# A new instruction order for the head of a fused attention and gated-FFN kernel: softmax of batch 0 by halves, other PSUM banks, three weight visits exchanged

## The chip, the core and the metric

The kernel runs on one core of a Trainium2 chip. The core has a matrix engine (TensorE, PE in the profile) and three others that work on tiles: VectorE (DVE), ScalarE (ACT) and GpSimd (POOL). SyncE (SP) issues transfers; ACT and POOL issue some too. Each engine takes its instructions in the order in which the program gives them to it, and waits at an instruction until what it reads is there and what it overwrites is no longer needed. The metric is the device time of one execution in microseconds (us); less is better.

## What is computed

Two stages. The first is a pair of cross attentions, for 8 batches and 8 heads, between x (512 rows of 64) and a state (32 rows of 64):

```
a     = softmax(scale * x  @ state^T);   xread = a  @ state
a2    = softmax(scale * state @ x^T);    sread = a2 @ x
y     = concat(xread, sread)             # 544 rows per batch, heads side by side: 4352 x 512
```

The second is a gated FFN over those rows, with 512 inner and 1536 hidden columns:

```
out = (sigmoid(y @ w_gate) * (y @ w_val)) @ w_out
```

## The kernel before, in words

The whole kernel is scheduled by hand: the order of the calls in the program is the order on each engine's queue, and the tile framework adds the waits. There are eight PSUM banks, each a pool with one buffer, named G0, G1, OU, S0, S1, S2, S3 and AT; a call takes the bank it is to write as an argument, and waits until the last reader of that bank is done.

Attention and FFN are fused. Since xread is a linear map of the softmax weights, the kernel multiplies the state with w_gate and w_val once per batch (a *visit*, `sw_visit` at L297: eight matmuls for 256 columns of both weights, or 512 columns of one, into two banks, halves e = 0 and 1), copies the result to SBUF as `SW` (`sw_cp` at L328), and then multiplies `SW` with the transposed weights `aT`. `sw_wide` (L311) makes three visits in a row for batch 2.

The names that the order speaks of, for a batch b:

- `load_xp`, `load_xh` load parts of x; `cast_xp` (L93) makes bf16 of it. `xT_mm` (L126) transposes x on TensorE into a bank, `xT_cp` (L134) copies it out. `warm` (L600) issues 128x512 matmuls on zeros that nobody reads.
- `sT_mm`, `sT_pad`, `sT_cp` (L621 to L639) transpose the state and copy it out.
- `Sq_mm`, `Sq_exp`, `nq_sum`, `nq_mul` (L170 to L194) are scores, exponentials, row sums with reciprocals, and the division, for a quarter of batch 0 (two heads). `S_mm`, `S_exp`, `n_sum`, `n_mul` (L142, L164, L206, L223) are the same for a half (four heads).
- `aT_mm` (L230) transposes the divided weights `ab` on TensorE, `aT_cp` copies them out; from batch 2 on `aT_dma` does it by transposing transfers on SP, and `at_xT_dma` (L137) does it for x.
- `at_Eb` (L196) makes bf16 of the exponentials on POOL, and `rd_mm` (L253) multiplies them with x for the second attention: 32 matmuls, and 8 with a column of ones for the row sums. `rd_fin` (L270) divides.
- `gv_mm(b, f, gate bank, value bank)` (L335) is a unit of the gated FFN: for 128 hidden columns, two matmuls for the gate and two for the value. `gv_half` (L350) is the one or the other alone. `gv_th` (L361) takes tanh of the gate on ACT into a tile `th`, of which there are three buffers, and `gv_glu` (L366) joins gate and value on DVE.
- `h_mm`, `h_sum`, `ht_sum` (L448, L464, L467) multiply the result for batch 0 with w_out in seven products of 2x2 blocks instead of eight, with sums of blocks made on DVE and POOL. `load_wo(q)` loads a third of w_out; every product reads all three thirds or sums of them.

The head of the program, from L650 to L924, works on batches 0 and 1 and prepares batch 2; this is the part that is laid out anew. Behind it, `step(b, f)` (L971) runs over batches 2 to 7 in a fixed pattern of twelve units each, and is not touched. `step` begins with three visits and then a half unit that writes bank G1.

Of the kernel before, what the change touches and what calls it, by code (L numbers as in the profile page):

```python
# [16 lines left out]
def kernel(  # L17
# [75 lines left out]
    def cast_xp(b, cp, lo, n):  # L93
        xh_tile(b)
        cp(xhs[b][:, lo:lo + n], xfs[b][:, lo:lo + n])
# [504 lines left out]
    def warm(n, place):  # L600

        ps = place[0].tile((128, 512), FP, name="warm", tag=place[1])
        for _ in range(n):
            nc.tensor.matmul(ps.rearrange("p (r k) -> p r k", r=4), wm, wm.unsqueeze(1).to_broadcast((128, 4, 128)), start=True, stop=True)  # L604
# [50 lines left out]
    nc.vector.memset(wm, 0.0)  # L655
# [23 lines left out]
    load_w(0, 256, 256)
    load_w(1, 256, 256)  # L680
    Sq_mm(0, 0, S2)
    load_w(0, 1024, 256)
    Sq_exp(0, 0)
    xT_cp(0, 1, vec)
    Sq_mm(0, 1, AT)
    xT_mm(0, 3, S3)
    xT_mm(1, 0, S0, 2)
    nq_sum(0, 2)
    load_w(1, 1024, 256)
    xT_cp(0, 3, act)  # L690
    load_sb(2)
    Sq_mm(0, 3, OU)
    Sq_exp(0, 1)
    nq_sum(0, 0)
    nq_sum(0, 1)
# [45 lines left out]
    sw_cp(1, 1024, 2, 0, act)
    aT_mm(1, S0)
    gv_glu(0, 3)
    aT_cp(1, None, vec)
    gv_mm(0, 2, S2, S1)
    gv_th(0, 2)
# [1 line left out]
    gv_mm(0, 9, AT, S3)
    gv_mm(1, 3, G1, S0)
    gv_th(0, 9)  # L750
    sw_cp(1, 1024, 2, 1, vec)
    gv_mm(1, 2, AT, G0)
    gv_glu(0, 9)
    gv_th(1, 3)
    gv_glu(1, 3)
    nc.scalar.activation(pre[:, 0:1], ones, AF.Exp)
    gv_th(1, 2)
    sT_mm(2, S1)
    gv_mm(1, 8, S2, S3)
    zero(sTz, pool)  # L760
    gv_th(1, 8)
    gv_glu(1, 2)
    load_x(2, nc.gpsimd)
# [70 lines left out]
    sw_cp(2, 1, 2, 0, act)
    h_sum(0, 1, vec)
    gv_mm(1, 6, OU, S3)
    sw_visit(1, 1280, 256, S1, G0)
# [2 lines left out]
    sw_visit(1, 0, 256, S2, S0)  # L840
    sw_cp(1, 1280, 2, 0, act)
    h_sum(2, 0, pool)
    h_sum(2, 1, vec)
    sw_cp(1, 1280, 2, 1, act)
    gv_mm(1, 4, G1, OU)
    gv_glu(1, 6)
    cast_x(2, pool, 0, 4)
    gv_mm(1, 7, S1, AT)
    gv_th(1, 4)
    sw_cp(1, 0, 2, 1, vec)  # L850
    gv_glu(1, 4)
# [2 lines left out]
    gv_mm(1, 11, S3, G1)
    h_sum(1, 1, pool)
    gv_th(1, 11)
    at_xT_dma(2)
    gv_mm(1, 10, G0, S1)
    gv_glu(1, 11)
    h_mm(1, 0, AT)  # L860
    h_mm(1, 1)
    ht_sum(0, vec)
    h_sum(0, 0, pool)
    h_mm(5, 0, G1)
    S_mm(2, 0, OU)
    h_mm(5, 1)
    ht_sum(2, vec)
    h_sum(1, 0, vec)
    load_x(3, nc.sync)
    ht_sum(1, vec)  # L870
    gv_th(1, 10)
    h_mm(7, 0, S0)
    gv_glu(1, 10)
    sw_cp(1, 0, 2, 0, act)
    h_sum(3, 0, pool)
    w_keep('V1', 1)
    h_mm(6, 0)
    S_exp(2, 0)
    n_sum(2, 0)
    n_mul(2, 0, pool)  # L880
    S_mm(2, 1, G0)
    aT_dma(2, 0)
    S_exp(2, 1)
    gv_mm(1, 0, OU, S2)
    h_sum(3, 1, vec)
    gv_th(1, 0)
    h_mm(6, 1)
    w_keep('U2', 1)
    n_sum(2, 1)
    ht_sum(3, vec)  # L890
    n_mul(2, 1, pool)
    aT_dma(2, 1)
    h_U4()
    gv_mm(1, 1, G0, S1)
    h_mm(2, 0, S3)
    gv_glu(1, 0)
    h_mm(2, 1)
    gv_th(1, 1)
    cast_x(3, pool, 4, 4)
    h_mm(3, 0)  # L900
    gv_glu(1, 1)
    cast_x(3, pool, 0, 4)
    at_xT_dma(3)
    h_mm(7, 1)
    w_add(2, 'V1', w_res(0, 0)[:, :, lo_])
    h_mm(3, 1)
    sw_wide(2, 0, AT, S2, S1, G0, S3, OU)
    w_add(7, 'U4', w_res(0, 1)[:, :, hi_])
    sw_cp(2, 0, 1, 1, act)
# [286 lines left out]
```

## Time and profile before

| what | value |
|---|---|
| time, median of 3 runs | 211.4 us (211.23 to 212.68) |
| the profiled execution, its own time | 211.41 us |
| its span, first to last instruction | 209.6 us |
| DVE, ACT, POOL busy, 25 to 30 us | 4.75, 4.30, 2.49 us of 5 |
| DVE, ACT, POOL busy, 40 to 45 us | 4.96, 2.44, 2.82 us of 5 |

The profile page gives the busy time of each engine and its share of the span, then the chain of work that ended last. A view by stage cuts the span into stretches: each row has the stretch, its length, and for each engine the busy time with its number of instructions, then the granted clock, the share of the transfer engines and GB/s. Rows of the timeline have start, duration, engine, source line, operation, what is written and read, and in brackets how long the engine stood idle before it and what ended that. A row of the timeline merges neighbours of one kind (x4), and its duration is then that of the group. Groups of instructions have count, busy time and mean nanoseconds of one. Rows of transfers have the issuing queue, the size and the microseconds from issue to landing.

A duration of a matmul includes its way through the array, so neighbours overlap: what a matmul costs in a dense stretch is the pitch from start to start.

### The profile page before, as it was taken

Reading aid. Unit: us, or ns where it says so; the run is one execution under the profiler, and the core shown is the slowest. Engines: PE = TensorE matmul, PEld = TensorE weight load, DVE = VectorE, ACT = ScalarE, POOL = GpSimd, SP = SyncE. Lnnn points to the kernel's source line nnn. Section 1 sums busy time; section 2 is a strip of 40 time slices with the busy share of each in tenths; the row PEclk is TensorE's granted clock in tenths of the full one; section 3 lists DMA queues with packets and bytes.
Section 4 is the critical chain, followed back from the end, with each engine's and each line's share of the span. In section 5 each row is a group of like instructions: output and inputs, shape, how many; then the busy total and the mean of one; then the engine's idle time right before and its main releaser. Section 6 shows DMA issues by size and latency. Waiting matters only on the chain.

```text
span 209.6 us, 5504 instructions
## 1 busy us (share of the span) xinstructions
PE 202.9 (97%) x2161; PEld 132.8 (63%) x2161; DVE 172.1 (82%) x332; ACT 136.0 (65%) x257; POOL 79.7 (38%) x104
## 2 busy tenths in 40 slices
PE   7879999999999999999999999999999999999993
PEld 2545443677666656665666575666666777778982
DVE  1798899998997788668979898898978779798962
ACT  3978898753867467865786478648787566565420
POOL 8899458599041704900292028501600000000010
PEclk9999999999999999999999999999999999999998
DMA  6999999672689952995913440275020500022045
GB/s 206 186 192 191 226 278 183 113 213 42 78 208 337 141 103 77 308 119 161 299 45 60 105 170 16 44 99 206 13 47 0 204 1 3 0 85 118 2 156 147
DMA packets 40922, 27.17 MB, mean 130 GB/s; under 512 B 23616, under 2 KB 38720, under 8 KB 40896
## 3 DMA queue, kind: packets, MB, share of 16 engines
q1 hardware_dynamic: 30000, 18.95, 36.0%
q0 software_dynamic: 9920, 7.01, 20.5%
q10 hardware_dynamic: 976, 0.85, 1.3%
q8 instruction: 17, 0.28, 0.6%
q14 instruction: 9, 0.07, 0.1%
HBM read 18.35 MB, written 8.91 MB: 130 GB/s over the span
## 4 chain that ended last, share of the span: by engine, by line
PE 94%; DVE 2%; ACT 2%; issue 0%
PE gvp L355 30%; PE outp L434 29%; PE gvp L343 10%; PE gvs L531 4%; PE outp L454 4%; PE swp L286 4%; PE swp L293 2%; PE outp L571 2%; PE warm L604 2%; PE Sp L147 1%; PE outp L479 1%; PE rdp L262 1%; DVE rsq L186 1%; PE aTp L234 1%; ACT tw L638 1%; PE rdp L265 1%
## 5 line engine op out<-in xcount | busy, mean ns | idle before, releaser
L369 DVE SCALAR_TENSOR_TENSOR glu<-th,gvp 128x512 bf16<-128x512 f32 x96 | 64.9, 682 | 23.1 <-PE gvp L355 10.6
L364 ACT ACTIVATE th<-gvp 128x512 f32<-128x512 f32 x96 | 57.5, 603 | 35.2 <-PE gvp L355 32.4
L355 PE MATMUL gvp<-aT,SW 128*128 128x512 bf16 x288 | 77.5, 380 | 0.0
L329 ACT CAST SW<-swp 128x512 bf16<-128x512 f32 x83 | 46.6, 594 | 9.2 <-PE swp L286 8.3
L434 PEld LDWEIGHTS <-Sm 128*128 128x128 bf16 x324 | 31.3, 98 | 11.1 <-DVE Sm L414 0.2
L355 PEld LDWEIGHTS <-SW 128*128 128x128 bf16 x288 | 26.7, 98 | 17.0 <-issue 3.3
L200 POOL CAST Eb<-E 128x256 bf16<-128x256 f32 x32 | 13.9, 473 | 52.1 <-ACT E L167 52.1
L434 PE MATMUL outp<-tw,Sm 128*128 128x256 bf16 x240 | 31.4, 273 | 0.0
L434 PEld LDWEIGHTS <-glu 128*128 128x128 bf16 x240 | 23.2, 98 | 9.4
L434 PE MATMUL outp<-wo,glu 128*128 128x256 bf16 x168 | 22.8, 273 | 0.0
L343 PE MATMUL gvp<-aT,SW 128*128 128x512 bf16 x96 | 22.6, 380 | 0.0
L596 POOL DMA_DIRECT2D out_dram<-res x1 | 0.6, 613 | 50.1 <-ACT res L442 50.1
L227 POOL TENSOR_TENSOR ab<-E,ri 128x512 bf16<-128x512 f32 x13 | 14.3, 1101 | 10.6 <-DVE ri L210 6.0
L414 DVE TENSOR_TENSOR Sm<-glu 128x768 bf16<-128x768 bf16 x30 | 16.6, 559 | 0.0
L343 PEld LDWEIGHTS <-SW 128*128 128x128 bf16 x96 | 8.7, 98 | 10.5 <-issue 1.9
L445 DVE SCALAR_TENSOR_TENSOR res<-outp,U 128x512 f32<-128x512 f32 x20 | 13.6, 684 | 0.9 <-PE outp L454 0.9
L116 POOL CAST xb<-xf 128x1024 bf16<-128x1024 f32 x12 | 13.2, 1122 | 2.0 <-DMA xf<-in_x_dram 2.0
L167 ACT ACTIVATE E<-Sp 128x512 f32<-128x512 f32 x14 | 8.4, 599 | 6.7 <-PE Sp L147 5.8
L434 PE MATMUL outp<-wo,Sm 128*128 128x256 bf16 x84 | 11.3, 273 | 0.0
L251 POOL CAST xs<-xf 128x1024 bf16<-128x1024 f32 x10 | 10.1, 1040 | 0.0
L434 PE MATMUL outp<-tw,glu 128*128 128x256 bf16 x72 | 9.8, 273 | 0.0
L208 DVE TENSOR_REDUCE rs<-E 128x16 f32<-128x512 f32 x14 | 9.5, 677 | 0.2 <-ACT E L167 0.2
(124 smaller groups left out, 262.4 us busy)
## 6 DMA issues: line engine op xcount, KB each, us to landing
out_dram<-res SPq DMA_DIRECT2D x14, 512.0 KB, 3.2
xf<-in_x_dram SPq DMA_DIRECT2D x5, 1024.0 KB, 7.6
wo<-in_moe_w_out_dram POOLq DMA_DIRECT2D x3, 512.0 KB, 7.9
wgv<-in_moe_w_gate_dram POOLq DMA_DIRECT2D x4, 256.0 KB, 7.0
wgv<-in_moe_w_val_dram POOLq DMA_DIRECT2D x4, 256.0 KB, 8.3
xf<-in_x_dram POOLq DMA_DIRECT2D x1, 1024.0 KB, 9.5
xf<-in_x_dram SPq DMA_DIRECT2D x2, 256.0 KB, 3.9
xf<-in_x_dram ACTq DMA_DIRECT2D x2, 256.0 KB, 4.4
```

Of the source, the lines that this page charges most:

```text
L116: cp(xbs[b].rearrange("p c h d -> p h c d")[:, lo:lo + n], (xhs if b in xhs else xfs)[b][:, lo:lo + n])
L200: nc.gpsimd.tensor_copy(Ebs[b][:, c], E1s[b][:, c])
L227: (nc.gpsimd if eng is pool else nc.vector).tensor_tensor(half(b, i, abs_), e1, ri.unsqueeze(len(ri.shape)).to_broadcast(e1.shape), ALU.mult)
L251: pool(xs.rearrange("p c h d -> p h c d")[:, lo:lo + n, :, :D], xfs[b][:, lo:lo + n])
L329: cp(*sw_left.pop((b, lo, w, e)))
L343: nc.tensor.matmul(ps, SWs[b][:, g, w, fs], aTs[b][:, :, g], start=(g == 0), stop=(g == 1))
L355: nc.tensor.matmul(ps, SWs[b][:, g, w, fs], aTs[b][:, :, g], start=(g == 0), stop=(g == 1))
L364: nc.scalar.activation(th, held["gv", b, f][0], AF.Tanh, scale=0.5)
L369: nc.vector.scalar_tensor_tensor(glus[b][:, f], held["th", b, f], 1.0, held["gv", b, f][1], ALU.add, ALU.mult)
L414: eng.tensor_tensor(S_(b, t)[:, i], a, c, op)
L434: nc.tensor.matmul(wps[key][:, c], lhs[:, i, c * 128:(c + 1) * 128], rhs[:, i], start=(first and c == 0 and i == 0), stop=(i == NF // 2 - ...
L445: nc.vector.scalar_tensor_tensor(to, wps[key], 0.5, held["w", name], ALU.mult, ALU.add)
```

## The change

The functions keep what they do, except that `rd_mm` now issues the eight matmuls with ones ahead of the 32 others for batch 2, and as before behind them for batches 0 and 1. Everything else is the order of calls in the head and the arguments that name engines and banks:

- Batch 0's softmax: sums, reciprocals and divisions by halves (`n_sum`, `n_mul`) instead of quarters (`nq_sum`, `nq_mul`); scores and exponentials stay by quarters, in the order 1, 0, 2, 3 instead of 2, 0, 1, 3 for the exponentials.
- Unread matmuls: 4 + 1 + 1 + 3 + 1 + 2, instead of 4 + 4 + 3.
- The visit of batch 1 at 256 lies before gv(0,3); the first half of gv(0,2) lies before the visits at 1024.
- `sw_visit(1, 512, 512, ...)` for both weights changes place with `sw_visit(1, 1280, 256, ...)` and `sw_visit(1, 0, 256, ...)`, and the gv units of batch 1 follow in another order.
- Many banks, and some copies between DVE and ACT, are exchanged. On POOL, `load_x(2)` is issued before sTz is cleared, `load_wo(1)` right behind `load_wo(0)`, and `load_wo(2)` behind `h_sum(2, 0, pool)`, with the second `cast_x(2)` behind that.
- The order of the h products, and the bank of rd(2): G1 instead of S2.

The core of the diff:

```diff
     load_xp(0, nc.sync, 0, 2)
     load_s(0, nc.scalar)
-    load_xp(0, nc.scalar, 4, 2)
-    load_xp(0, nc.sync, 2, 2)
-    load_xp(0, nc.scalar, 6, 2)
+    zero(sbz, pool)
+    make_identity(nc, ident)
+    load_xh(1, 0, 4)
     nc.vector.memset(wm, 0.0)
     warm(4, S1)
-    zero(sbz, pool)
-    warm(4, S1)
...
+    cast_s(0, vec)
+    load_xp(0, nc.scalar, 2, 2)
+    load_xp(0, nc.scalar, 6, 2)
+    warm(1, S1)
+    cast_xp(0, act, 0, 2)
+    load_xp(0, nc.sync, 4, 2)
+    zero(sTd, vec)
+    sT_mm(0, S2)
+    sT_pad(1, act)
...
+    xT_mm(0, 3, S1)
+    Sq_mm(0, 1, AT)
+    Sq_exp(0, 1)
+    Sq_exp(0, 0)
...
+    n_sum(0, 0)
+    n_mul(0, 0, pool)
+    xT_mm(1, 0, S3, 2)
     Sq_exp(0, 2)
+    Sq_exp(0, 3)
+    at_Eb(0, 0)
+    warm(3, S1)
...
+    xT_mm(1, 2, S2, 2)
+    load_w(1, 1280, 256)
+    xT_cp(1, 2, act, 2)
+    S_mm(1, 0, S0)
+    warm(1, OU)
     S_exp(1, 0)
+    n_sum(0, 1)
+    n_mul(0, 1, vec)
+    aT_mm(0, G1)
+    aT_cp(0, 0, act)
     n_sum(1, 0)
+    at_Eb(0, 1)
     S_mm(1, 1, S2)
+    warm(2, OU)
+    S_exp(1, 1)
     load_w(0, 1280, 256)
+    sw_visit(0, 256, 256, G0, OU)
+    sw_cp(0, 256, 2, 0, vec)
     aT_cp(0, 1, act)
+    load_w(0, 0, 256)
+    sw_cp(0, 256, 2, 1, act)
+    sw_visit(1, 256, 256, S0, S3)
...
+    gv_mm(0, 3, G0, OU)
+    gv_half(0, 2, 0, G1)
     gv_th(0, 3)
+    sw_visit(0, 1024, 256, S3, AT)
...
+    gv_mm(0, 9, S3, AT)
+    gv_th(0, 9)
+    gv_th(0, 2)
+    gv_mm(1, 3, S2, S1)
...
+    gv_mm(1, 2, G1, G0)
+    gv_glu(0, 9)
+    gv_mm(1, 8, S2, S3)
+    gv_glu(1, 3)
+    gv_th(1, 2)
+    gv_glu(1, 2)
+    nc.scalar.activation(pre[:, 0:1], ones, AF.Exp)
+    gv_th(1, 8)
...
+    gv_mm(0, 8, S0, G0)
     gv_glu(0, 2)
+    sT_cp(2, act)
+    gv_th(0, 8)
     sw_visit(0, 0, 256, AT, S2)
...
-    sw_visit(1, 512, 512, S3, S1, 0)
-    sw_visit(0, 512, 512, OU, S0, 1)
...
+    sw_visit(1, 1280, 256, S3, S0)
+    sw_visit(1, 0, 256, AT, G0)
...
-    cast_x(2, pool, 4, 4)
-    load_wo(2)
...
+    sw_wide(2, 1, S3, OU, S0, S1, S2, AT)
...
+    h_sum(2, 0, pool)
...
+    load_wo(2)
...
+    cast_x(2, pool, 4, 4)
+    h_sum(1, 1, pool)
     ht_sum(0, vec)
+    h_mm(1, 1)
+    at_xT_dma(2)
...
+    S_mm(2, 0, OU)
...
+    h_mm(2, 0, S3)
...
+    h_mm(5, 0, G1)
...
+    S_mm(2, 1, S2)
```

More of the change, by code (lines that the diff above doesn't have):

```diff
@@ L251, in cast_xs, with rd_ones @@
         pool(xs.rearrange("p c h d -> p h c d")[:, lo:lo + n, :, :D], xfs[b][:, lo:lo + n])
+    def rd_ones(b, rd):
+        for e in range(2):
+            for c in range(4):
+                nc.tensor.matmul(rd[:, e, D:], Ebs[b][:, c, e], ones, start=(c == 0), stop=(c == 3))
     def rd_mm(b, place):
@@ L265, in rd_mm @@
                         nc.tensor.matmul(o[:, :D], Eb, xh, start=(c == 0), stop=(c == 3))
-        for e in range(2 if b < 3 else 0):
-            for c in range(4):
-                nc.tensor.matmul(rd[:, e, D:], Ebs[b][:, c, e], ones, start=(c == 0), stop=(c == 3))
+        if b < 2:
+            rd_ones(b, rd)
     def rd_fin(b):
@@ L675 @@
-    xT_cp(0, 2, act)
-    cast_xp(0, act, 6, 2)
-    Sq_mm(0, 2, S1)
-    Sq_exp(0, 2)
[L679 to L695, printed above, removed]
+    load_xh(1, 4, 4)
+    load_w(0, 256, 256)
+    xT_cp(0, 1, vec)
@@ L741 @@
[L741 to L746, printed above, removed]
-    gv_glu(0, 2)
[L748 to L763, printed above, removed]
@@ L764 @@
-    gv_mm(0, 8, S0, G0)
+    sw_visit(0, 1024, 256, S3, AT)
+    sw_cp(0, 1024, 2, 0, act)
+    sw_visit(1, 1024, 256, S0, G0)
+    sw_cp(0, 1024, 2, 1, act)
+    aT_mm(1, S2)
+    gv_glu(0, 3)
+    aT_cp(1, 0, vec)
+    gv_half(0, 2, 1, OU)
+    aT_cp(1, 1, act)
+    load_w(0, 512, 512)
+    gv_mm(0, 9, S3, AT)
+    gv_th(0, 9)
+    gv_th(0, 2)
+    gv_mm(1, 3, S2, S1)
+    sw_cp(1, 1024, 2, 0, vec)
+    sw_cp(1, 1024, 2, 1, vec)
+    load_w(1, 512, 512)
+    gv_th(1, 3)
+    gv_mm(1, 2, G1, G0)
@@ L789 @@
-    gv_glu(0, 8)
+    sT_cp(1, vec)
+    gv_mm(0, 10, G0, S3)
     gv_th(0, 10)
-    pad(2, 6)
+    load_x(2, nc.gpsimd)
+    zero(sTz, pool)
     gv_glu(0, 0)
     gv_glu(0, 10)
+    sw_visit(0, 512, 512, AT, OU, 0)
+    load_wo(0)
+    load_wo(1)
     sw_cp(0, 512, 0, 0, act)
     gv_mm(0, 11, S2, G1)
-    sw_visit(1, 512, 512, S3, S1, 0)
-    sw_visit(0, 512, 512, OU, S0, 1)
+    gv_th(0, 11)
+    sw_visit(1, 1280, 256, S3, S0)
+    sw_visit(1, 0, 256, AT, G0)
+    sw_cp(1, 1280, 2, 0, act)
@@ L826 @@
+    sw_wide(2, 1, S3, OU, S0, S1, S2, AT)
+    gv_th(0, 6)
+    gv_mm(1, 11, G0, G1)
+    cast_x(2, pool, 0, 4)
+    gv_glu(0, 4)
     gv_glu(0, 6)
-    sw_cp(2, 1, 0, 1, act)
     sw_cp(2, 1, 0, 0, vec)
     sw_cp(2, 1, 1, 1, vec)
+    sw_cp(2, 1, 0, 1, act)
+    gv_mm(1, 10, OU, S3)
+    h_sum(2, 0, pool)
     sw_cp(2, 1, 1, 0, act)
-    gv_mm(1, 5, S1, G1)
+    gv_th(1, 11)
+    gv_glu(1, 11)
+    sw_cp(2, 1, 2, 1, act)
+    sw_visit(1, 512, 512, S1, G0, 0)
+    h_sum(0, 1, vec)
+    gv_th(1, 10)
@@ new lines @@
+    h_sum(2, 1, vec)
+    sw_visit(1, 512, 512, AT, G1, 1)
+    gv_glu(1, 10)
+    sw_cp(1, 512, 1, 1, vec)
+    sw_cp(1, 512, 0, 0, act)
+    sw_cp(1, 512, 1, 0, act)
+    sw_cp(1, 512, 0, 1, act)
+    gv_mm(1, 1, S0, OU)
+    load_wo(2)
+    gv_th(1, 1)
+    gv_mm(1, 0, S1, AT)
+    gv_glu(1, 1)
+    gv_mm(1, 4, S3, G1)
+    gv_mm(1, 5, G0, S1)
+    h_mm(1, 0, AT)
+    gv_th(1, 0)
+    gv_glu(1, 0)
+    cast_x(2, pool, 4, 4)
+    h_sum(1, 1, pool)
+    ht_sum(0, vec)
+    h_mm(1, 1)
+    at_xT_dma(2)
@@ L832 @@
+    gv_th(1, 4)
+    gv_glu(1, 4)
+    S_mm(2, 0, OU)
+    sw_cp(2, 1, 2, 0, act)
+    ht_sum(2, vec)
+    h_mm(2, 0, S3)
+    h_sum(0, 0, pool)
+    h_mm(5, 0, G1)
+    h_sum(1, 0, vec)
+    h_sum(3, 0, pool)
+    w_keep('V1', 1)
     gv_th(1, 5)
+    S_exp(2, 0)
+    S_mm(2, 1, S2)
+    h_mm(5, 1)
+    load_x(3, nc.sync)
     gv_glu(1, 5)
[L834 to L837, printed above, removed]
-    gv_th(1, 6)
-    sw_cp(2, 1, 2, 1, act)
@@ L840 @@
[L840 to L851, printed above, removed]
+    gv_mm(1, 6, G0, S1)
+    ht_sum(1, vec)
+    h_sum(3, 1, vec)
+    n_sum(2, 0)
+    n_mul(2, 0, pool)
+    aT_dma(2, 0)
+    S_exp(2, 1)
+    h_mm(6, 1)
+    h_mm(6, 0)
+    n_sum(2, 1)
+    n_mul(2, 1, pool)
@@ L852 @@
+    gv_th(1, 6)
+    ht_sum(3, vec)
+    h_mm(7, 0, S0)
+    w_keep('U2', 1)
+    h_U4()
+    h_mm(2, 1)
+    w_add(2, 'V1', w_res(0, 0)[:, :, lo_])
+    gv_mm(1, 7, OU, G0)
+    h_mm(7, 1)
+    h_mm(3, 0)
     gv_th(1, 7)
     gv_glu(1, 7)
[L854 to L909, printed above, removed]
+    sw_wide(2, 0, S3, S2, AT, OU, S1, G0)
     sw_cp(2, 0, 0, 1, act)
     sw_cp(2, 0, 2, 0, act)
+    gv_glu(1, 6)
@@ L912 @@
+    sw_cp(2, 0, 0, 0, act)
+    at_Eb(2)
+    h_mm(3, 1)
+    w_add(7, 'U4', w_res(0, 1)[:, :, hi_])
+    h_mm(4, 0)
+    cast_x(3, pool, 0, 4)
+    aT_dma(2, 1)
+    cast_x(3, pool, 4, 4)
+    at_xT_dma(3)
+    sw_cp(2, 0, 1, 0, act)
+    h_mm(4, 1)
+    sw_cp(2, 0, 1, 1, vec)
     w_add(5, 'U2', w_res(0, 0)[:, :, hi_])
     w_store(0, 0, nc.sync)
-    h_mm(4, 0)
+    sw_cp(2, 0, 2, 1, act)
+    rd_mm(2, G1)
+    w_add(7, 'U2', w_res(0, 1)[:, :, lo_])
     load_x(4, nc.sync)
-    sw_cp(2, 0, 0, 0, act)
```

127 lines of the change are left out of this document (47 added, 80 removed).

## The prediction

> **What bounds the kernel now.** I read the page first, for the share of each engine and the chain that ended last; then busy time by stage, to see where TensorE is not full; then the chain in order of time; then the timeline of the head and the rows of the two stretches that are laid out anew.
>
> ```profile
> span 209.6 us, 5504 instructions
> ...
> PE 202.9 (97%) x2161; PEld 132.8 (63%) x2161; DVE 172.1 (82%) x332; ACT 136.0 (65%) x257; POOL 79.7 (38%) x104
> ...
> PE 94%; DVE 2%; ACT 2%; issue 0%
> ```
>
> ```profile
> 5.00:10.00 5.00, 4.33 (x55) 3.08 (x56) 3.52 (x11) 4.25 (x10) 4.38 (x7) 1.00 1.31 195
> 10.00:15.00 5.00, 3.68 (x91) 2.50 (x89) 4.60 (x11) 3.72 (x7) 4.98 (x10) 1.00 1.52 191
> 15.00:20.00 5.00, 5.00 (x43) 2.26 (x42) 3.99 (x8) 4.56 (x11) 5.00 (x10) 1.00 1.50 194
> ...
> 50.00:55.00 5.00, 5.00 (x111) 3.08 (x88) 4.06 (x9) 4.53 (x9) 2.73 (x5) 1.00 0.43 79
> ```
>
> The chain is TensorE (94%), and by stage TensorE is full from 15 us on (5.00 of 5.00). The change moves matmuls about but leaves every matmul that is read. So the end can move in three ways only: the full stretch begins earlier, new gaps open in it, or matmuls run at another speed. Before 15 us TensorE is short 0.67 us in one stage and 1.32 us in the next, and part of what it does there is read by nobody. That bounds the gain.
>
> ```profile
> 16.72 3.45 PE gvp L343 x16
> 20.40 1.73 PE gvp L343 x8
> 22.13 0.56 PE swp L293 x16
> ...
> 39.67 1.97 PE outp L454 x18
> ```
>
> These pieces of the chain price TensorE work: a 128x512 matmul 3.45/16 = 0.216 us, so a gv unit (four) 0.86 and a half unit 0.43; a visit (eight small matmuls) 0.28; an h product (six) 1.97/3 = 0.66.
>
> **The change, part by part.** First the head, up to the first gv unit, gv(0,3).
>
> ```profile
> 7.30 0.62 ACT L95 CAST xf<-xf 128x512 bf16<-128x512 f32 x1
> 7.46 0.52 PE L174 MATMUL Sp<-tw,xT 128*128 128x64 bf16 x12 [0.41 <-ACT xT L135]
> 7.82 0.66 ACT L182 ACTIVATE E<-Sp 128x256 f32<-128x256 f32 x2
> ...
> 10.53 1.05 DVE L193 TENSOR_TENSOR ab<-E,riq 128x256 bf16<-128x256 f32 x2
> ...
> 11.72 0.61 PE L234 MATMUL aTp<-ident,ab 128*128 128x128 bf16 x8 [0.59 <-DVE ab L193]
> 12.10 0.67 DVE L208 TENSOR_REDUCE rs<-E 128x16 f32<-128x512 f32 x1
> ...
> 12.36 1.07 ACT L244 COPY aT<-aTp 128x512 bf16<-128x512 bf16 x2 [0.60 <-PE aTp L234]
> ...
> 12.80 0.25 DVE L210 RECIPROCAL ri<-rs 128x16 f32<-128x16 f32 x1
> ...
> 13.32 0.62 ACT L167 ACTIVATE E<-Sp 128x512 f32<-128x512 f32 x1
> 13.81 0.61 ACT L329 CAST SW<-swp 128x512 bf16<-128x512 f32 x1
> ...
> 14.47 1.04 PE L343 MATMUL gvp<-aT,SW 128*128 128x512 bf16 x4
> 15.11 0.60 ACT L364 ACTIVATE th<-gvp 128x512 f32<-128x512 f32 x1
> 15.21 0.68 DVE L227 TENSOR_TENSOR ab<-E,ri 128x512 bf16<-128x512 f32 x1
> ```
>
> The gap before aT_mm (0.59, released by DVE's ab) is what the halves aim at. New working: the last part of x(0), heads 6 and 7, is cast at 7.30 without a DMA wait, so it has landed by then. In the new order ACT is free earlier and waits for it; I put the landing at 7.0 (bounds: 7.30 above; 5.3 below, where the earlier parts land). Cast to 7.62. Now Sq(0,1) stands behind xT(0,3), which needs that cast, and Sq_exp(0,0) stands behind Sq_exp(0,1): four transposes 0.25, then 0.36 from Sq to its exponential (7.46 to 7.82), then two exponentials of 0.33: about 8.9. Each half is 0.67 + 0.25 and a handoff on DVE (about 0.97), two of them 10.85, then the multiply of the second half 0.68: aT_mm at 11.55 instead of 11.72. POOL's multiply of the first half lies beside it. Then ACT ends the head: copy of aT 0.64 after aT_mm starts (11.72 to 12.36), at 12.2; S_exp(1,1), the second half of aT and the copy of the first visit follow at a pitch of 0.49 (13.32 to 13.81), the last takes 0.61: 14.28. So **gv(0,3) starts at 14.3 instead of 14.47**, and the second visit (0.28) and rd(0) lie before it, rd without its old wait for the aT bank. Lead: 0.17 + 0.28 = **0.45 us**. The unread matmuls (11 before, 12 after, five of them first) lie in idle stretches: nothing, as long as the clock is the same (a rival, below). The loads of x(0) change places between SP and ACT in pairs, the same bytes at the same places in the queues: nothing. POOL's issues of the weights up to 8.2 us are the same.
>
> Next, 14.3 to gv(1,9). TensorE's work to the start of gv(1,2) is four gv units, one of them in halves, 3.45, two visits 0.56, aT_mm 0.55: 14.3 + 4.55 = 18.85. Small waits come in: the G0 bank is free only after th(0,3), which stands behind three copies on ACT; gv(0,9) needs the copy on ACT after that; gv(1,2) needs bank G1, freed by th(0,2), now queued behind th(0,9). About 0.17 in all: 19.0. Before, gv(1,2) is the fourth unit after 16.55, at 19.15. The lead is down to **0.15**.
>
> ```profile
> 16.55 3.62 PE L343 MATMUL gvp<-aT,SW 128*128 128x512 bf16 x16
> ...
> 19.39 1.87 DVE L369 SCALAR_TENSOR_TENSOR glu<-th,gvp 128x512 bf16<-128x512 f32 x3
> ...
> 22.62 1.90 PE L343 MATMUL gvp<-aT,SW 128*128 128x512 bf16 x8
> ...
> 25.45 0.60 ACT L364 ACTIVATE th<-gvp 128x512 f32<-128x512 f32 x1 [0.29 <-DVE glu L369]
> ```
>
> The last row shows a wait that exists already: th has three buffers, so a th waits for the glu of three th's before. In the new order th(1,8) waits so for glu(0,2), which now stands on DVE behind glu(1,2). Let gv(1,2) start at P. th(1,2) starts 0.64 later (14.47 to 15.11), takes 0.60; glu(1,2) at P+1.27; glu(0,2) at a pitch of 1.87/3 = 0.62, ending P+2.55; th(1,8) P+2.6 to 3.2. It frees bank S2 for the visit (0,0). TensorE's work up to there is gv(1,2), gv(1,8), the state transposes (0.23 by the chain's step from 16.72+3.45 to 20.40) and gv(0,8): P+2.8. **A gap of 0.4.** Behind th(1,8) on ACT stand the copy of the state transposes and th(0,8), P+3.45 to 4.05, which frees S0 for gv(1,9) at P+4.1, while the two visits end at P+3.8. **A gap of 0.3.** So gv(1,9) starts at 23.1; before, 22.62: **lag 0.5**. If DVE and ACT run at their shortest pitches these gaps halve; if glu(0,9) is late, they grow: 0.3 to 1.0.
>
> From there to the wide visit the banks come free in time by the same steps, but for the second wide pair, whose S1 (instead of G0) waits for th(0,6), about 0.1: lag **0.6**. The exchange of visits (1,512) with (1,0) and (1,1280) is four visits for four, two here and two there, at 0.28 each: nothing. DVE takes the copies of (1,1024) e0 from ACT, 0.68, behind it aT_cp and glu(0,9): counted in the 19.0.
>
> Then the h products. Here load_wo(2), the last third of w_out, moves on POOL's queue from before h_sum(2,0) to behind it, and the second cast of x(2) and with it the transposes of x(2) on SP behind that.
>
> ```profile
> 31.01 1.04 POOL L116 CAST xb<-xf 128x1024 bf16<-128x1024 f32 x1 [1.98 <-DMA xf<-in_x_dram]
> 31.99 0.74 POOL L107 DMA_DIRECT2D wo<-in_moe_w_out_dram  x1
> 33.05 1.64 POOL L414 TENSOR_TENSOR Sm<-glu 128x768 bf16<-128x768 bf16 x1 [0.32 <-DVE glu L369]
> ...
> 35.70 5.21 SPq L140 DMA_TRANSPOSE xT<-xb  x4
> ...
> 39.50 1.47 PE L454 MATMUL outp<-wo,glu 128*128 128x256 bf16 x12
> ```
>
> ```profile
> wo<-in_moe_w_out_dram POOLq DMA_DIRECT2D x1, 512.0 KB, 6.4
> ...
> xT<-xb SPq DMA_TRANSPOSE x2, 2.5
> ...
> out_dram<-res POOLq DMA_DIRECT2D x1, 512.0 KB, 4.1
> ```
>
> h_sum waits for glu(0,4) (33.05 before), with the lag 33.5, and takes 1.64: wo(2) is issued at 35.1 instead of 31.99. It lands 4.1 to 6.4 later (the one queued behind other loads, as here before; the other alone on the queue): 39.2 to 41.5. h_mm(1,0) starts at 39.5 + 0.6 = 40.1 and reads wo(2) with its fifth matmul, at 40.5. I take 40.3, nearer the lone transfer, since wo(1) is now issued four us earlier: no wait, with 0 to 1.0 kept for the range. By the Trainium skill, "DMA: Bandwidth & Descriptors", Anatomy of one DMA (about 2 us and 436 KB per us), this transfer would land some 3.2 us after its descriptors are written, an estimate; that too would be in time. The second cast then runs 35.9 to 36.95, and the four transposes are issued at a pitch of 5.21/4 = 1.3: the last at 40.85, landing 2.5 later, 43.35. S(2,1) comes after h(1,0), h(1,1), S(2,0), h(2,0), h(5,0): 40.1 + 4 x 0.66 + 0.2 = 42.95. **A gap of 0.4.** Lag **1.0**. After it ht_sum(1), the aT transposes and rd_fin(2) (whose bank G1 the next step now needs) come within 0.2 of TensorE in my working, covered by the h products and by 0.84 us of visits; if that cover is gone each costs its excess. rd(2) takes its eight matmuls with ones ahead of the others instead of behind: the same eight, nothing. POOL clears sTz behind the issue of x(2) instead of before; pad waits for the state copies anyhow, and x(2) waits for the queue (the 1.98 on POOL): nothing.
>
> **The sum.** -0.45 in the head, +0.3, +0.65 and +0.1 up to the wide visit, +0.4 at the transposes: +1.0 us. The profiled execution took 211.41 us (span 209.6, 1.8 around it), the median is 211.4. Forecast **212.4 us**.
>
> **The rivals.**
>
> ```profile
> 0.99 3.81 PE L604 MATMUL warm<-wm 128*128 128x512 bf16 x8 [0.99 <-DVE wm L655]
> ```
>
> ```profile
> L132 PE MATMUL xTp<-ident,xf 128*128 128x128 bf16 x6 | 1.0, 310 | 0.0
> L132 PE MATMUL xTp<-ident,xf 128*128 128x128 bf16 x8 | 0.9, 282 | 0.0
> L132 PE MATMUL xTp<-ident,xf 128*128 128x128 bf16 x8 | 0.6, 220 | 0.0
> ```
>
> 1. **The clock comes up late** (slower). The three rows are transposes at 5.9 to 6.4, 6.4 to 7.1 and 7.9 to 8.4 us: 310 ns, mixed, 220 ns. TensorE runs slowly until about 6.8 and fast after, having been busy from 0.99 almost without a break. The granted clock shows 1.00 throughout and tells nothing of this. In the new order TensorE stands idle from about 3.4 to 4.0 and 5.5 to 6.1. If the slow stretch lasts to about 10, three unread matmuls at 0.43 (their pitch in the first row) instead of 0.22 delay xT(1,2) by 0.65, of which some 0.5 reaches gv(0,3): 212.9. If it lasts into the gv units, to 17 us, the PE work from 14.3 on runs at half speed, 1.35 us lost, and 0.3 more in the head: **214.5**, slower by over 1%. It decides from the point where the slow clock reaches about 15.3 (213.5). Chance 0.3, of which 0.13 for the long form. The rule beside it is in the Trainium skill, "TensorE: Matmul & The Clock Gate", Parts 1 and 4: half clock until a free-running window of some 3.4 us was busy, and transposes do not count as busy. The trace agrees with the first as far as a switch at about 6.8 goes (310 to 220 ns); the second no run here shows.
> 2. **The gaps do not come** (faster). If th(1,8) and the transposes are in time, only the lead is left: 211.4 - 0.45 = **210.95**, and 210.6 if the landing of x(0) is earlier than 7.0 by 0.35. For it: the order before has hardly a gap on TensorE after 15 us. Against: the th buffers and the SP pitch are in the rows. Chance 0.2. Faster by 1% would need gv(0,3) at about 12.6, before the ACT chain above has begun its copies.
> 3. **wo(2) lands late**: at 41.5, h_mm(1,0) waits 1.0 and swallows the 0.4 at the transposes: **213.0**; with the ht_sum behind it late as well, 213.8. Chance 0.1.
>
> **Chances and range.** Forecast 0.4, the clock 0.3, no gaps 0.2, w_out 0.1. About 1% is what a measurement of this kernel can tell from no change: 209.3 and 213.5 are the limits. Slower: 0.13 from the clock, 0.02 from w_out, 0.03 from the forecast's own tail: 0.18. Faster: 0.03. Within: 0.79. The range runs from the second rival's lower value, 210.6, to just short of the long slow clock, 214.2.
>
> **What would show it.** aT_mm at 11.55 and gv(0,3) at 14.3; a th waiting for DVE's glu near 20 to 22 and the visit (0,0) behind it; gv(1,9) at 23.1; the issue of w_out's last part behind h_sum at 35; S(2,1) waiting for the SP transposes at 43.4; transposes of x(1) at 220 ns if the clock is up by then. Wrong would be: TensorE full from 14.3 to 55 (rival 2), transposes or gv matmuls at the slow duration after 10 us (rival 1), or a gap of some us that I have not named.

## The result, and the profile after

| | before | after |
|---|---|---|
| time, median | 211.41 us (211.23 to 212.68, 4 runs) | 214.94 us (214.73 to 215.2, 4 runs) |
| profiled execution, its span | 211.41, 209.6 us | 215.01, 213.2 us |
| start of gv(0,3) | 14.47 | 14.96 |
| start of aT_mm(1) | 16.10 | 17.26 |
| start of gv(1,9) | 22.62 | 23.46 |
| first unit of `step` on the chain | 53.35 | 56.77 |

Before aT_mm(1) the new order has half a gv unit more (0.43 us), so 1.16 us later there is 0.73 for the same work.

The ratio is 1.0160, 95% interval 1.0127 to 1.0193: slower by 1.6%, where 212.4 was forecast and the range ended at 214.2. The span grew by 3.6 us, and 3.4 of them are there when `step` begins (56.77 against 53.35): the loss was made in the part that was laid out anew.

From the page of after: the busy times, and the engines' shares of the chain that ended last.

```profile
span 213.2 us, 5494 instructions
...
PE 205.3 (96%) x2162; PEld 134.1 (63%) x2162; DVE 174.2 (82%) x328; ACT 136.8 (64%) x257; POOL 80.0 (38%) x103
...
PE 85%; DVE 6%; DMA 4%; issue 1%; POOL 1%; ACT 0%; ACTq 0%; DVEq 0%
```

Before, the chain was 94% TensorE. Now DVE, a transfer and POOL hold 11% of it. The busy time by stage of after says where TensorE stands:

```profile
40.00:45.00 5.00, 5.00 (x52) 3.88 (x51) 4.13 (x7) 2.85 (x6) 1.86 (x2) 1.00 0.91 155
45.00:50.00 5.00, 3.82 (x31) 2.85 (x30) 4.93 (x8) 1.36 (x3) 2.69 (x3) 1.00 0.57 188
```

In the stage 45 to 50 TensorE (first busy column) works 3.82 of 5 us and DVE (third) 4.93: DVE has become the bound of the h products. In the stage before, DVE has a hole (4.13). The chain of after in order of time (start, length, what) shows what made the hole:

```profile
18.36 3.52 PE gvp L349 x16
...
22.97 0.56 PE swp L299 x16
...
33.39 0.70 DVE glu L375
34.17 1.59 POOL Sm L420
35.76 5.13 DMA wo<-in_moe_w_out_dram
...
45.24 1.94 DVE tw L413
```

glu(0,4), then POOL's sum h_sum(2,0), then the transfer of w_out's last part that is issued behind that sum, then DVE's sums of w_out blocks (`tw`), one of them 1.94 us long. From issue to landing that transfer took, by the rows of the transfers into `wo` after 30 us:

```profile
DMA to landing us min/median/max: 5.8/5.8/5.8
```

so it landed at 41.56, and DVE took up its first sum at 41.75. The timeline of after has the same instructions with the engine beside them:

```profile
8.99 1.04 PE L132 MATMUL xTp<-ident,xf 128*128 128x128 bf16 x8
...
11.11 0.62 PE L132 MATMUL xTp<-ident,xf 128*128 128x128 bf16 x8
...
15.49 1.07 POOL L227 TENSOR_TENSOR ab<-E,ri 128x512 bf16<-128x512 f32 x1
...
16.04 1.07 DVE L227 TENSOR_TENSOR ab<-E,ri 128x512 bf16<-128x512 f32 x1
...
41.75 0.96 DVE L413 TENSOR_TENSOR tw<-wo 128x1536 bf16<-128x1536 bf16 x1 [0.86 <-issue]
...
44.14 0.40 PE L147 MATMUL Sp<-sTz,xT 128*128 128x64 bf16 x8
...
44.73 1.64 POOL L420 TENSOR_TENSOR Sm<-glu,Sm 128x768 bf16<-128x768 bf16 x1 [3.13 <-DVE Sm L420]
...
45.16 2.02 DVE L413 TENSOR_TENSOR tw<-wo,tw 128x1536 bf16<-128x1536 bf16 x1
...
47.24 2.12 PE L460 MATMUL outp<-tw,Sm 128*128 128x256 bf16 x18 [1.18 <-DVE tw L413]
```

Three things are to be seen. Transposes are still slow at 8.99 (eight in 1.04 us) and fast only at 11.11 (0.62), where before they were fast from 7.98. DVE's multiply n_mul(1,1) took 1.07 us beside POOL's n_mul(1,0); before, it took 0.68 with POOL done. And DVE's ht_sum(1) took 2.02 us beside POOL's h_sum(3,0), where the row before it of the same size took 0.96; TensorE waited 1.18 us for it. DVE's 4.93 busy us above count such a stretched instruction in full, so part of them is standing.

### The profile page after: what moved, and what is told of

Read it like the earlier page. It is cut to its first block, busy times and chain, and to the rows that moved or that the text cites. A ratio compares the mean times of both kernels' runs of the same rounds, so it can differ in the third digit from the quotient of the medians.

```text
span 213.2 us, 5494 instructions
## 1 busy us (share of the span) xinstructions
PE 205.3 (96%) x2162; PEld 134.1 (63%) x2162; DVE 174.2 (82%) x328; ACT 136.8 (64%) x257; POOL 80.0 (38%) x103
## 4 chain that ended last, share of the span: by engine, by line
PE 85%; DVE 6%; DMA 4%; issue 1%; POOL 1%; ACT 0%; ACTq 0%; DVEq 0%
PE gvp L361 30%; PE outp L440 29%; PE gvp L349 6%; PE gvs L537 4%; PE swp L292 3%; DMA wo<-in_moe_w_out_dram 2%; PE swp L299 2%; PE outp L577 2%; DMA xf<-in_x_dram 2%; DVE tw L413 2%; DVE glu L375 2%; PE xTp L132 1%; PE outp L485 1%; PE Sp L147 1%; PE warm L610 1%
## 5 line engine op out<-in xcount | busy, mean ns | idle before, releaser
L335 ACT CAST SW<-swp 128x512 bf16<-128x512 f32 x82 | 46.0, 591 | 8.2 <-PE swp L292 6.9
L200 POOL CAST Eb<-E 128x256 bf16<-128x256 f32 x32 | 14.7, 496 | 51.3 <-ACT E L167 51.3
L227 POOL TENSOR_TENSOR ab<-E,ri 128x512 bf16<-128x512 f32 x14 | 15.4, 1102 | 14.0 <-DVE ri L210 9.5
L420 DVE TENSOR_TENSOR Sm<-glu 128x768 bf16<-128x768 bf16 x30 | 17.7, 594 | 0.0
L208 DVE TENSOR_REDUCE rs<-E 128x16 f32<-128x512 f32 x16 | 10.7, 671 | 1.9 <-ACT E L167 1.4
```

The lines of the kernel that those rows point to most:

```text
L200: nc.gpsimd.tensor_copy(Ebs[b][:, c], E1s[b][:, c])
L208: nc.vector.tensor_reduce(grp(b, rs), half(b, i, E1s), AX.X, ALU.add)
L227: (nc.gpsimd if eng is pool else nc.vector).tensor_tensor(half(b, i, abs_), e1, ri.unsqueeze(len(ri.shape)).to_broadcast(e1.shape), ALU.mult)
L335: cp(*sw_left.pop((b, lo, w, e)))
L420: eng.tensor_tensor(S_(b, t)[:, i], a, c, op)
```

## The experiments

The theory after this reading had four parts: w_out's last part comes late to DVE's sums (W); TensorE's clock comes up late (C); POOL's and DVE's operations get in each other's way in the head (H) and in the h products (P). The rivals were that one of them carries the whole loss, or that gaps at the th buffers do, as the prediction had it.

### w_out's last part ahead of the sum (e1), and late in the kernel before (e4)

In after:

```diff
     cast_x(2, pool, 0, 4)
+    load_wo(2)
     gv_glu(0, 4)
...
-    load_wo(2)
     gv_th(1, 1)
```

> The changed kernel with one line moved: the last third of w_out is issued on POOL ahead of h_sum(2,0) instead of behind it; the second cast of x(2) stays behind h_sum. Theory W (the late w_out costs the second half of the loss: it lands at 41.6, the DVE sums that need it start at 41.75 instead of 39.7, and DVE leads TensorE until 53): the transfer lands near 38.5, the first sum over w_out starts by 40.5, TensorE's wait of 1.2 us for a sum over w_out is gone, rd(2) ends near 54.0 instead of 56.0, time about 213.0 us. Rival D (the new order of the h products and of DVE's work, and collisions of DVE with POOL, cost it whenever w_out lands): rd(2) still ends after 55.3, time 214.3 or more.

213.85 us (213.82 to 213.88), ratio 1.0105 (1.0072 to 1.0138): 1.1 us of the 3.5 come back, a little over half of what was expected. The timeline of this kernel shows what took the place of the wait:

```profile
39.08 1.65 POOL L420 TENSOR_TENSOR Sm<-glu 128x768 bf16<-128x768 bf16 x1
...
40.25 1.30 DVE L413 TENSOR_TENSOR tw<-wo 128x1536 bf16<-128x1536 bf16 x1
...
43.56 1.64 POOL L420 TENSOR_TENSOR Sm<-glu,Sm 128x768 bf16<-128x768 bf16 x1 [2.83 <-DVE Sm L420]
...
44.00 2.02 DVE L413 TENSOR_TENSOR tw<-wo,tw 128x1536 bf16<-128x1536 bf16 x1
```

w_out is there, DVE starts 1.5 us earlier, and two of its sums still run into POOL's: 1.30 and 2.02 us instead of 0.95. A third, ht_sum(3), took 1.26 us beside POOL's division for batch 2 (0.90 in before).

The same order of POOL's queue, put into before:

```diff
-    cast_x(2, pool, 4, 4)
-    load_wo(2)
...
+    cast_x(2, pool, 0, 4)
     h_sum(2, 0, pool)
+    load_wo(2)
+    cast_x(2, pool, 4, 4)
...
-    cast_x(2, pool, 0, 4)
```

> The kernel before with POOL's order at this place as in the changed kernel: first half of x(2) cast, h_sum(2,0), the last third of w_out, second half of x(2), and nothing else changed. W: w_out's last part is issued near 34.7 instead of 32.0 and lands near 40.5, DVE's sums start 0.8 to 1.0 late and the transposes of x(2) on SP too, so the time is 1.0 to 2.0 us more, 212.4 to 213.4 us. D: no more than 0.4 us, 211.8 or less, since the old order of the h products hides it.

212.3 us (212.0 to 213.72, 10 runs), ratio 1.0056 (1.0031 to 1.0082): 0.9 us. TensorE's wait list of this kernel has the transfer itself with 0.3 us, and its chain passes through the transfer:

```profile
PE outp L454 <- DMA wo<-in_moe_w_out_dram: 0.3, 1, 0.3
```

So this order of POOL's queue is worth about 1 us in both kernels. In e4 a part of it is TensorE's own wait; in after the wait list has no wait of TensorE for a transfer, and the loss came by way of DVE, whose sums read w_out.

The edit moves a second thing, though. The second cast of x(2) on POOL stands behind the load, and the issue of the load (0.79 us) pushes it onto two of DVE's sums of glu's results, h_sum(0,1) and h_sum(2,1). The timeline of after:

```profile
36.55 1.06 POOL L116 CAST xb<-xf 128x1024 bf16<-128x1024 f32 x1
...
36.57 1.93 DVE L420 TENSOR_TENSOR Sm<-glu 128x768 bf16<-128x768 bf16 x2
```

and the same two sums in e1:

```profile
36.52 1.11 DVE L420 TENSOR_TENSOR Sm<-glu 128x768 bf16<-128x768 bf16 x2
```

In before they took 1.02 us, in e4 1.82. The first h product started at 41.04 in after and at 40.50 in e1, a difference made before the transfer landed. An estimate from these rows: with w_out there in time, DVE's first sum over it could have begun at 40.9 in after, beside POOL's sum of 39.96 to 41.59, and ended near 42.4. It ended at 42.71, and in e1 at 41.55. So most of the gain of e1 may be the cast's and not the landing's; no run here moves one without the other.

### The clock's gaps filled (e2), and both (e3)

```diff
+    warm(1, AT)
     xT_mm(0, 0, G1)
+    warm(1, AT)
     xT_mm(0, 1, S1)
```

> The changed kernel with two more unread 128x512 matmuls, one ahead of and one behind the first transposes of x(0), in TensorE's idle gaps between 4.5 and 6.2 us. Theory C (the gaps in the first 6 us keep TensorE at the slow clock until about 10.7): transposes of x(1) at 9 us take 220 ns instead of 312, gv(0,3) starts 0.3 to 0.6 us earlier than 14.96, time 0.3 to 0.7 us less, 214.4. Rival (the clock comes up by its own time, whatever fills these gaps): transposes still 310 ns at 9 us, gv(0,3) at 15.0 or up to 0.2 later, 214.9 to 215.1.

214.74 us (214.17 to 215.05), ratio 1.0141 (1.0097 to 1.0185). The clock did come up earlier: the eight transposes that start between 8.5 and 9.0 us take 1.04 us in each profile with the gaps left (after, e1, e5, e6, e11), and with them filled 0.61 in e2, e3 and e7 and 0.90 in e8. gv(0,3) started at 14.50 instead of 14.96; but aT_mm(1) hardly moved (17.14). Timeline of this kernel:

```profile
8.90 0.61 PE L132 MATMUL xTp<-ident,xf 128*128 128x128 bf16 x8
...
15.37 1.07 POOL L227 TENSOR_TENSOR ab<-E,ri 128x512 bf16<-128x512 f32 x1
...
15.60 1.40 DVE L227 TENSOR_TENSOR ab<-E,ri 128x512 bf16<-128x512 f32 x1
...
17.14 0.61 PE L234 MATMUL aTp<-ident,ab 128*128 128x128 bf16 x8 [0.54 <-DVE ab L227]
```

POOL's multiply is held at 15.4 by a weight load that stands ahead of it on POOL's queue. DVE now reaches its own multiply sooner, and is held for longer: 1.40 us. The lead ends there. In the profiles of after, e1, e2, e5 and e6 aT_mm(1) always starts between 17.14 and 17.26, while gv(0,3) starts anywhere from 14.50 to 14.96.

> Both edits together. W and C both right and independent: the gains add, about 212.4 to 212.6 us, still a little slower than before (211.4) since the small waits at banks between gv(0,3) and gv(1,9) stay. If the gain of one is hidden by the other: 213.0 (W alone) or 214.4 (C alone).

213.85 us (213.55 to 214.27), ratio 1.0107 (1.0071 to 1.0142): the same as e1, so filling the gaps alone is worth nothing that can be measured.

### POOL's multiply ahead of its weight load (e7), and that alone (e11)

```diff
-    load_w(0, 0, 256)
...
     n_mul(1, 0, pool)
+    load_w(0, 0, 256)
```

With e3's edits:

> E3 (w_out early, gaps filled) with POOL's multiply n_mul(1,0) issued ahead of the load of w_gate's first columns instead of behind. Theory P in the head (DVE's n_mul(1,1) takes 1.1 to 1.4 us instead of 0.68 since POOL's multiply runs beside it, and this sets aT(1) at 17.2): POOL's multiply runs 0.75 earlier, DVE's takes 0.7 to 0.9, the transposes of aT(1) start 0.3 to 0.6 earlier than in E3, time 213.3 to 213.6. Rival: the transposes of aT(1) wait for TensorE's or ACT's own chain, or the gain is absorbed at the h products: 213.7 or more.

213.02 us (212.72 to 213.13), ratio 1.0080 (1.0061 to 1.0098): 0.83 less than e3. Timeline:

```profile
7.17 0.61 PE L132 MATMUL xTp<-ident,xf 128*128 128x128 bf16 x8
...
14.14 1.06 POOL L227 TENSOR_TENSOR ab<-E,ri 128x512 bf16<-128x512 f32 x1
...
15.13 0.68 DVE L227 TENSOR_TENSOR ab<-E,ri 128x512 bf16<-128x512 f32 x1
...
16.07 0.62 PE L234 MATMUL aTp<-ident,ab 128*128 128x128 bf16 x8
```

POOL is done when DVE starts, the multiply takes 0.68 us, and aT_mm(1) starts at 16.07, no later than before, with half a gv unit more done. In this profile the clock came up earlier than in e2's, too (gv(0,3) at 14.04), so not all of the shift in it is the edit's.

Without the filled gaps (e1 and this edit):

> After with w_out's last part loaded ahead of the sum (e1, 213.85), and load_w(0, 0, 256) moved behind POOL's multiply n_mul(1, 0); the gaps are not filled, so the clock comes up late as in after. Theory A (slow clock and the collision of the two multiplies are two separate delays in a row, the later one hides the earlier): the collision is gone, n_mul(1,1) takes 0.68, but aT_mm(1) then waits for what the slow clock delays (gv(0,3) at 14.9): aT_mm(1) at 16.5 to 16.9 instead of 17.26, time 213.4 to 213.6. Rival B (the collision was the whole loss of the head, the clock costs nothing): aT_mm(1) at 16.1 and 213.0, as with both edits. Rival C (the order of POOL's queue does not matter while the clock is late): 213.85 within 0.1.

214.13 us (213.92 to 214.23), ratio 1.0129 (1.0114 to 1.0144): no gain over e1. Timeline:

```profile
11.10 1.06 PE L132 MATMUL xTp<-ident,xf 128*128 128x128 bf16 x8
...
16.47 0.68 DVE L227 TENSOR_TENSOR ab<-E,ri 128x512 bf16<-128x512 f32 x1
...
17.53 0.62 PE L234 MATMUL aTp<-ident,ab 128*128 128x128 bf16 x8
```

The collision is gone (0.68), but in this profile the clock came up still later than in after (gv(0,3) at 15.39 instead of 14.96), and everything behind it is later by as much. So H hides C, as e2 shows: with the gaps filled alone nothing is gained. That C hides H likewise rests on e11 alone, whose clock was later than after's; what the edit gives with the clock of after is not shown. Only both edits together were seen to gain.

### One glu behind the sum (e5)

e1 with

```diff
-    gv_glu(1, 5)
     gv_mm(1, 6, G0, S1)
     ht_sum(1, vec)
+    gv_glu(1, 5)
```

> E1 (w_out early) with one DVE instruction moved: glu(1,5) behind the second sum over w_out, ht_sum(1), instead of ahead of it. Theory P (a DVE operation that starts while POOL works on a tensor operation stands until POOL is done; glu(1,5) let POOL's h_sum(3,0) start first at 43.56, so ht_sum(1) took 2.02 us instead of 0.95): now ht_sum(1) starts first, takes 0.95, POOL's h_sum(3,0) is the one that is stretched (2.3 as before the change), TensorE's wait of 0.8 us for it is gone, time 0.6 to 1.0 us less than E1: 213.0. Rival D (DVE simply has too much to do before ht_sum(1) whatever its order, and the 2.02 us is not POOL's doing): ht_sum(1) still takes 1.5 or more, time 213.6 or more.

213.74 us (213.64 to 213.8), ratio 1.0110 (1.0092 to 1.0128): 0.1 less than e1. Timeline:

```profile
43.44 0.94 DVE L413 TENSOR_TENSOR tw<-wo,tw 128x1536 bf16<-128x1536 bf16 x1
...
43.59 2.29 POOL L420 TENSOR_TENSOR Sm<-glu,Sm 128x768 bf16<-128x768 bf16 x1 [2.83 <-DVE Sm L420]
...
44.30 0.68 DVE L375 SCALAR_TENSOR_TENSOR glu<-th,gvp 128x512 bf16<-128x512 f32 x1
44.90 1.39 DVE L420 TENSOR_TENSOR Sm<-glu,Sm 128x768 bf16<-128x768 bf16 x1
```

The durations turned round as the theory has it: whoever starts first runs at its own pace (DVE 0.94), the other is stretched (POOL 2.29 instead of 1.64). But the next sum on DVE then hit the same POOL row (1.39), and the wide visit waited 0.42 us for a glu. The time did not come back, it moved. The glu between them, which reads PSUM, kept its 0.68 beside POOL.

### The old order of the h products (e6)

e1, with the order, the banks and the engines of before from the first h product to rd_fin(2), 47 lines out and 47 in; of the h products and what feeds them:

```diff
-    h_mm(1, 0, AT)
...
-    ht_sum(0, vec)
-    h_mm(1, 1)
...
+    gv_mm(1, 5, G0, S1)
     gv_glu(1, 4)
...
+    h_mm(1, 0, AT)
+    h_mm(1, 1)
+    ht_sum(0, vec)
     h_sum(0, 0, pool)
     h_mm(5, 0, G1)
+    S_mm(2, 0, OU)
+    h_mm(5, 1)
+    ht_sum(2, vec)
     h_sum(1, 0, vec)
+    load_x(3, nc.sync)
+    ht_sum(1, vec)
...
     h_sum(3, 0, pool)
```

> E1 with the old order of the h products, of DVE's sums and of banks from h(1,0) on (gv units of batch 1 renamed to those that are left; the same work). Theory H (what E1 leaves of the loss behind the first h product, about 1.5 us, is this order): rd(2) ends about 1.0 us later than before the change instead of 2.5, time 212.3 to 212.6. Rival (the loss there is carried in from the head or from w_out and any order shows it): 213.4 or more.

212.43 us (212.04 to 212.44), ratio 1.0045 (1.0029 to 1.0061): 1.4 less than e1. The stretch 38 to 56 us by stage, first of e1, then of this kernel:

```profile
38.00:56.00 18.00, 16.96 (x212) 11.92 (x211) 17.00 (x27) 9.84 (x20) 12.46 (x13) 1.00 0.44 111
```

```profile
38.00:56.00 18.00, 18.00 (x220) 12.79 (x219) 16.64 (x30) 11.03 (x22) 13.18 (x13) 1.00 0.47 119
```

TensorE is full again, with DVE busy for 0.4 us less. In this order ht_sum(1) starts 0.17 us ahead of POOL's h_sum(3,0), and it is POOL that is stretched. Timeline of this kernel:

```profile
43.08 0.96 DVE L413 TENSOR_TENSOR tw<-wo,tw 128x1536 bf16<-128x1536 bf16 x1
...
43.25 2.29 POOL L420 TENSOR_TENSOR Sm<-glu,Sm 128x768 bf16<-128x768 bf16 x1 [2.49 <-DVE Sm L420]
```

None of DVE's four sums over w_out is stretched: together they take some 3.7 us, as in before, against 5.5 in e1 and 5.2 in after.

### Everything together (e8), and one unread matmul more (e9)

e7 with e6's order:

> The new head with all four edits: w_out early, gaps filled, POOL's multiply earlier, old order from the first h product on. If W, C, P and H hold and add: 211.7 to 212.1 us, that is, the new head alone is worth no gain over the old one (211.4). If the head edits carry through fully and its lead of one visit shows: 211.0 to 211.4. If they are absorbed: 212.5 or more.

211.86 us (211.28 to 211.95, 10 runs), ratio 1.0000 (0.9972 to 1.0028): the loss is gone.

```diff
-    warm(1, S1)
+    warm(2, S1)
     cast_xp(0, act, 0, 2)
```

> The kernel of e8 (after, with w_out's last part loaded ahead of the sum, both gaps filled, POOL's multiply ahead of its weight issue, and the old order of the h products) with one unread matmul more behind the first four (two instead of one), which fills TensorE from about 3.4 to 4.1 us. If the time at which the fast matmuls begin (about 8.5 us in e8's profile, 6.8 in before's) still costs something in the head, the fast transposes begin at about 7 to 7.5, gv(0,3) at 14.2 instead of 14.6, and the time is 211.2 to 211.6 against before's 211.4: a new head worth about what the prediction gave it, at most 0.45 faster. If the clock costs nothing once POOL's multiply is early, it stays at 211.86 within 0.15. What remains of the loss beyond that would then lie in the middle, between gv(1,9) and the wide visit.

211.16 us (211.03 to 212.31, 12 runs), ratio 0.9996 (0.9987 to 1.0006). gv(0,3) starts at 13.85, but against before this is no difference that can be measured. Timeline:

```profile
13.85 1.04 PE L349 MATMUL gvp<-aT,SW 128*128 128x512 bf16 x4
```

### The two delays of the head, put into before (e10, e12)

Three unread matmuls fewer:

```diff
     warm(4, S1)
     zero(sbz, pool)
-    warm(4, S1)
+    warm(1, S1)
```

> Before, with three unread matmuls fewer in its first run of them (four and one instead of four and four), so that TensorE stands idle from about 3.4 us to the first transposes, nothing else changed. The matmuls left out are read by nobody. Theory C (the time at which the matmuls become fast has a price of its own, whatever the order): transposes at 310 ns until about 10 us, Sq and xT later by 0.3 to 0.7, gv(0,3) at 14.8 to 15.2 instead of 14.47, and the kernel 0.3 to 0.7 us slower: 211.7 to 212.1. Rival: ACT and DVE set the pace of the old head (0.59 of idle ahead of its aT_mm), so that slow transposes are hidden: 211.4 within 0.15.

211.69 us (211.31 to 212.7, 12 runs), ratio 1.0017 (1.0003 to 1.0031): 0.3 us, at the lower end. The chain of this kernel has aT_mm(1) 0.29 later than before's (16.17), and everything behind it by as much:

```profile
16.46 0.55 PE aTp L234 x8
```

POOL's multiply late:

```diff
+    load_w(0, 0, 256)
+    load_sb(1)
     n_mul(1, 0, pool)
     rd_fin(0)
-    load_w(0, 0, 256)
-    load_sb(1)
```

> Before, with two weight and state loads of POOL's queue, load_w(0, 0, 256) and load_sb(1), issued ahead of POOL's multiply n_mul(1, 0) instead of behind it; nothing else changed, the fast matmuls begin early as in before. POOL's multiply then runs from about 15.1 to 16.2 us instead of 13.64 to 14.7, beside DVE's n_mul(1, 1) at 15.21. Theory D (a DVE operation on two SBUF operands and a POOL operation exclude each other, the later one stands until the first is done): one of the two takes about 1 us more (DVE 1.6 to 1.7 instead of 0.68, or POOL 1.7 instead of 1.06), aT_mm(1) starts at 16.6 to 16.9 instead of 16.10, and the kernel is 0.4 to 0.8 us slower: 211.8 to 212.2. Rival (they do not exclude each other; a late POOL multiply costs by its own end alone): DVE's row stays at 0.68, POOL's at 1.06, aT_mm(1) waits for POOL to about 16.2, and the time is 211.4 to 211.6.

212.19 us (211.62 to 212.44, 12 runs) against 211.48 of before beside it, ratio 1.0028 (1.0011 to 1.0045). Timeline:

```profile
14.90 1.06 POOL L227 TENSOR_TENSOR ab<-E,ri 128x512 bf16<-128x512 f32 x1
15.00 1.72 DVE L227 TENSOR_TENSOR ab<-E,ri 128x512 bf16<-128x512 f32 x1
...
16.86 0.61 PE L234 MATMUL aTp<-ident,ab 128*128 128x128 bf16 x8 [0.91 <-DVE ab L227]
```

POOL ends at 14.90 + 1.06 = 15.96, and 0.68 later, at 16.64, DVE could be done if it had stood until then; it ends at 16.72. A sharing of something between them would have stretched both; here only the later one is longer.

## Why the prediction was wrong

By the medians: 214.94, w_out early 213.85 (-1.1), the old h order 212.43 (-1.4), the head's edits 211.16 (-1.3), against 211.4 before. Step by step these are the 3.8 us between after and e9; inside the head the shares overlap, as shown. The forecast's terms added up to 1.0 us, and 3.5 came.

- **The head** was to lead by 0.45 and lagged by 0.49 (14.96 against 14.47). The step that failed is "the unread matmuls lie in idle stretches: nothing, as long as the clock is the same". The clock wasn't: rival 1's short form came, and with the gaps filled gv(0,3) started 0.46 earlier, near its price of 0.5. A second step was a misreading: 0.28 of the lead was to come from the second visit ahead of gv(0,3), but in before that visit stands there too:

```profile
14.12 0.41 PE L293 MATMUL swp<-wgv,tw 64*32 64x512 bf16 x8
```

  The sum takes this 0.28 out again, since it goes on from the two times at gv(1,2), 19.0 and 19.15; rival 2's 210.95 and the lower end of the range keep it. The halves had a small cost of their own: DVE's n_mul(0,1) took 0.89 us at 11.05 beside POOL's n_mul(0,0), which the working let lie beside it for nothing, and no run removes this. With the clock up early the new head does gain: e9 has gv(0,3) at 13.85 and gv(1,9) at 22.10, 0.52 ahead of before.
- **Up to gv(1,9)** the prediction had a fall from a lead to a lag of 0.5, by two gaps of th buffers and banks. The lag was 0.84, with another cause: 0.49 of it is there at gv(0,3), and the other 0.35 came in small pieces. The working let POOL's and DVE's multiplies for batch 1 lie beside each other for nothing. They put aT_mm(1) at 17.2 however early gv(0,3) was; in after the clock had TensorE so late that at most 0.14 more was lost there (0.80 us from the visits to aT_mm(1), 0.66 in before), and in e2 TensorE waited 0.54. e12 prices the collision at 0.7 us in the kernel before, where nothing hides it. The gaps of 0.4 and 0.3 did not appear: from 18.36 to 23.5 us the chain of after is TensorE's without a break.
- **w_out's last part** was to be issued at 35.1 and to land at 40.3, no wait. It was issued at 35.76, behind a sum that was itself late, and landed 5.8 us later (6.0 in e4), 41.56, the upper end of the range given; the estimate of 3.2 us in the prediction was far off. Rival 3 had this landing, at 213.0, or 213.8 with the sums behind it late. The order of POOL's queue cost what that rival gave to the wait (1.0; 1.1 in e1, 0.9 in e4), but not by it. Two steps failed: taking the h product as the reader that counts, where DVE's ht_sum(0) reads w_out too and started when it had landed; and pricing the later cast by its transposes alone, where it stretched DVE's sums beside it by 0.9 us. How the 1.1 us is shared between the two is open.
- **The transposes of x(2)** were to hold S(2,1) until 43.4. S(2,1) ran at 44.14 without a wait: TensorE itself was late by then.
- **The h products** are the largest miss. Behind S(2,1) the prediction put ht_sum(1) "within 0.2 of TensorE", covered, and priced the new order at nothing. It costs 1.4 us by e6. No place where a DVE sum falls on a POOL operation was priced. In before's timeline ht_sum(1) starts 0.16 us ahead of POOL's h_sum(3,0), and POOL's sum is the one that is stretched:

```profile
41.90 0.95 DVE L407 TENSOR_TENSOR tw<-wo,tw 128x1536 bf16<-128x1536 bf16 x1
...
42.06 2.29 POOL L414 TENSOR_TENSOR Sm<-glu,Sm 128x768 bf16<-128x768 bf16 x1 [2.39 <-DVE Sm L414]
```

  In the new order POOL starts first, ht_sum(1) takes 2.02, ht_sum(3) 1.26, and DVE becomes the chain. The sum of a rival or two (212.4 and 0.5 and 0.6) would not have reached 214.9 without this term. That the stretched sums are the whole of the 1.4 us is argued from the rows: e6 also moves banks and other work, and e5, which changed one of these meetings, gained 0.1.

What stays open: which of e6's many moves makes the order good. e5 shows that moving one instruction does not. Open too is where e9's lead of 0.52 at gv(1,9) goes: 0.26 of it is left when `step`'s first unit starts (53.02 against 53.28 by the timelines), and none can be measured in the time. Also open is why the clock came up later in e11 than in after, with the same instructions on TensorE up to there.

## What to carry to other kernels

Where an order puts a DVE operation on two SBUF operands beside a POOL operation that reads SBUF, count the later one from the end of the earlier, not from its own start; a table of both engines' queues with start and end shows such places before they are built. Ask of a transfer that is moved not only which matmul reads it, but which sums do, and how full their engine is. An idle stretch in a head's first microseconds is not free while the clock has yet to come up, and a delay there can hide a second one, so that either edit alone shows nothing.
